# Parts of q and k written by the compute engines straight into the score tiles

## The chip, the cores and the metric

The kernel runs on one core of one Trainium2 chip. The metric is the device time of one execution in microseconds. A core has five engines that run their own in-order queues beside each other: TensorE (PE in the profile, with PEld for its weight loads), VectorE (DVE), ScalarE (ACT), GpSimd (POOL) and SyncE (SP), which here issues all DMA transfers.

## The reference

Attention with rotary embedding, then two MLPs, all in float32:

```python
# q, k, v: batch 4, heads 8, seq 576, head_dim 64
q_rot, k_rot = rotate(q), rotate(k)   # x1*cos - x2*sin, x1*sin + x2*cos
scores = (1 / sqrt(64)) * q_rot @ k_rot.T
attn = softmax(scores)                # over keys, 1e-9 added to the sum
x = (attn @ v) as [2304 tokens, 512]
h = x @ w_in                          # w_in 512 x 2048
g = where(h >= 1, h, where(h <= -1, 0, (h + 1)**2 / 4))
x = g @ w_out                         # w_out 2048 x 512
r = maximum(x @ w_in2, 0)
out = (s * r * r + b) @ w_out2
```

## The kernel before

**Two parts for each number.** TensorE multiplies in a format that rounds float32 (`F32R`). So each operand is split into a high part, the value rounded to that format, and a low part, the rest, and a product is the sum of three: high by high, high by low, low by high.

**Pairs.** Two heads make a pair (`NPAIR` = 16). One head has 64 rows (its head dimension), so a pair's q and k lie in 128 rows, head 0 in rows 0 to 63 (`D` = 64) and head 1 in rows 64 to 127. Columns are the 576 positions. `load_qk` brings q or k of a pair into a tile `qin` or `kin` (one tag, four buffers) as two planes: the value and the value with its halves swapped. `rope_pair` multiplies both planes with the table (L240), adds them (L242), and makes the high part into plane 0 (ScalarE, L244 for q with the factor 1/8, L247 for k) and the low part into plane 1 (L245 on VectorE for q, L248 for k). The products are GpSimd's, except those of the first two pairs' q and the first pair's k; the sum is VectorE's for q and GpSimd's for k (VectorE's for the first k). `pool_tt` cuts GpSimd's work into pieces of at most 300 columns.

**The stacks.** A score matmul contracts over all 128 rows. For each head j the tile `qs` holds q's high part in 64 rows and its low part in the other 64, `kh` holds k's high part twice, once in each half, and `kz` holds k's low part against q's high part and zeros against q's low part. So `kh` by `qs` gives two of the three products in one pass, and `kz` by `qs` the third. `stack` fills these tiles with transfers from SBUF to SBUF of 64 rows by 576 columns: four for q (L259), six for k (L266). There are two `qs`, two `kz` and two buffers of `kh`, so the tiles of pair i + 2 are those of pair i.

**Units.** A pair has nine score tiles (units). For each, `qk` runs the score matmuls into one of two PSUM tiles `sc` (L287), VectorE takes the negated maximum `nm` (L289), and ScalarE the exp `p` (L294) with its sum. `tmain` and `trem` transpose `p` on TensorE and copy it back to SBUF, `finish` multiplies with v and with the inverse sums. `do_load` prepares later pairs: at unit 0 of pair i it traces `rope_pair` for q of pair i + 1, at unit 2 that for k, at units 4 and 6 the loads of pair i + 2.

**Order.** A scheduler of the framework orders each engine's queue beforehand, from a planned timeline; the engines then run their queues in order and wait on semaphores. `tc.issue_after(first)` keeps what is traced under it behind the instruction `first` in its engine's queue: the loads of pair 1 and all that SyncE issues for the first 36 units stand behind the last transfer of the first pair's stacks.

**Around it.** While attention runs, `do_fill` puts parts of the first MLP (`beside`: tiles `h`, `y`) between the units from unit 48 on, and `convert` splits weights (tiles `wraw`, `wa`, `wm`, `w`). The rest of both MLPs follows in `stage` (tiles `hps`, `yps`).

## Time and profile before

| | |
|---|---|
| median of 3 runs | 1181.76 us (1180.75 to 1182.14) |
| the profiled execution | 1180.8 us, its span 1179.0 us |
| TensorE busy | 1116.0 us, 95% of the span |
| ScalarE, VectorE, GpSimd busy | 681.2, 591.5, 557.4 us |
| mean granted TensorE clock | 0.984 of full speed |

The span runs from the first to the last instruction; times in the trace count from its start. Attention's last score matmuls run at about 460 us. Busy shares are averages over stages with different limits, so they are read by stage. "Idle before" an instruction is the idle time of its engine ahead of it, with what ended it. A granted clock of 1.00 is TensorE's 2.4 GHz level, 0.50 its 1.2 GHz level.

### The profile page before, as it was taken

What the parts mean: (1) busy time and instruction counts of PE and PEld (TensorE: products, weight loads), DVE (VectorE), ACT (ScalarE), POOL (GpSimd) and SP (SyncE); (2) the same over time, 40 slices, a digit from 0 to 9 for tenths busy, and PEclk for the clock granted to TensorE, in tenths of its full rate; (3) what the DMA queues carried; (4) which work ended last, traced back from release to release, by engine and by line L of the source; (5) the groups of instructions that cost most, each with busy time, mean ns of one, the idle gap of its engine ahead of it and who ended that gap; (6) DMA issues with size and microseconds to landing.
All of it is one profiled execution on the core that took longest, in us unless ns stands there. A gap on an engine that the chain in (4) does not pass through costs nothing.

```text
span 1179.0 us, 18887 instructions
## 1 busy us (share of the span) xinstructions
PE 1116.0 (95%) x6816; PEld 1001.7 (85%) x6816; DVE 591.5 (50%) x1013; ACT 681.2 (58%) x1431; POOL 557.4 (47%) x712
## 2 busy tenths in 40 slices
PE   3889899899999999999999889999999999999998
PEld 3667677788888888998999889999888889988887
DVE  4769887776554454466655656654411111211221
ACT  2657666655665655566655545567755646555553
POOL 3977987684433110567678887466611110111000
PEclk9989899999999999999999999999999999999999
DMA  7867656655444410433345463444302111312220
GB/s 222 231 179 223 184 156 197 189 159 159 133 141 117 113 52 32 146 118 123 112 154 156 129 179 120 135 135 130 123 33 64 50 41 40 97 33 74 65 65 33
DMA packets 73853, 142.67 MB, mean 121 GB/s; under 512 B 9504, under 2 KB 47392, under 8 KB 73760
## 3 DMA queue, kind: packets, MB, share of 16 engines
q1 hardware_dynamic: 73760, 141.46, 40.2%
q8 instruction: 54, 0.88, 0.3%
q14 instruction: 39, 0.32, 0.1%
HBM read 91.29 MB, written 26.54 MB: 100 GB/s over the span
## 4 chain that ended last, share of the span: by engine, by line
PE 60%; POOL 14%; DMA 7%; issue 6%; DVE 5%; ACT 4%; SPq 3%; POOLq 0%; ACTq 0%; DVEq 0%
PE hps L144 20%; PE yps L574 7%; PE yps L575 7%; PE yps L573 7%; PE sc L287 4%; PE h L144 4%; PE y L144 3%; POOL wm L86 3%; DMA xs<-xd 3%; PE av L335 3%; PE tp L309 3%; POOL kin L86 3%; POOL w L86 3%; POOL xl L86 2%; POOL qin L86 2%
## 5 line engine op out<-in xcount | busy, mean ns | idle before, releaser
L144 PE MATMUL hps<-xh,w 128*128 128x464 f32 (+5 forms) x1216 | 344.6, 349 | 0.8 <-POOL w L86 0.8
L86 POOL TENSOR_TENSOR xl<-xs,xh 128x232 fp32r<-128x232 f32 (+5 forms) x172 | 133.4, 801 | 271.7 <-ACT xh L90 270.5
L144 PEld LDWEIGHTS hps<-xh,w 128*128 128x128 f32 x1216 | 221.8, 188 | 16.0 <-POOL w L86 1.1
L573 PE MATMUL yps<-gh,w 128*128 128x464 f32 (+5 forms) x608 | 213.4, 351 | 4.6 <-ACT yo L580 4.2
L574 PE MATMUL yps<-gl,w 128*128 128x464 f32 (+5 forms) x608 | 212.7, 350 | 5.0 <-DVE gl L94 5.0
L575 PE MATMUL yps<-gh,w 128*128 128x464 f32 (+5 forms) x608 | 212.5, 350 | 0.0
L144 PE MATMUL hps<-xl,w 128*128 128x464 f32 (+5 forms) x608 | 211.5, 348 | 0.5 <-POOL xl L86 0.5
L94 DVE TENSOR_TENSOR gl<-ar,gh 128x464 fp32r<-128x464 f32 (+1 forms) x80 | 56.7, 709 | 268.7 <-ACT gh L90 268.6
L86 POOL TENSOR_TENSOR wm<-wm,w 128x256 f32<-128x256 f32 x128 | 114.8, 917 | 116.5 <-ACT w L131 60.7
L287 PE MATMUL sc<-kh,qs 128*128 128x288 f32 (+2 forms) x384 | 114.1, 332 | 42.3 <-ACT p L294 24.5
L289 DVE TENSOR_REDUCE nm<-sc 128x1 f32<-128x576 f32 x144 | 107.7, 753 | 79.8 <-PE sc L287 79.6
L573 PEld LDWEIGHTS yps<-gh,w 128*128 128x128 f32 x608 | 114.5, 188 | 14.6 <-ACT yo L580 6.3
L574 PEld LDWEIGHTS yps<-gl,w 128*128 128x128 f32 x608 | 114.6, 189 | 13.5 <-DVE gl L94 5.9
L144 PEld LDWEIGHTS hps<-xl,w 128*128 128x128 f32 x608 | 114.3, 188 | 8.3 <-POOL xl L86 0.7
L575 PEld LDWEIGHTS yps<-gh,w 128*128 128x128 f32 x608 | 114.6, 189 | 7.5
L294 ACT ACTIVATE p<-sc,nm 128x576 f32<-128x576 f32 x144 | 106.9, 745 | 23.5 <-DVE nm L289 22.7
L287 PEld LDWEIGHTS sc<-kh,qs 128*128 128x128 f32 x384 | 73.5, 204 | 54.4 <-ACT p L294 32.6
L175 ACT ACTIVATE ar<-hps 128x464 f32<-128x464 f32 (+1 forms) x80 | 44.4, 555 | 129.7 <-PE hps L144 129.7
L287 PE MATMUL sc<-kz,qs 128*128 128x288 f32 (+2 forms) x384 | 102.5, 303 | 0.0
L86 POOL TENSOR_TENSOR w<-wm,wa 128x256 fp32r<-128x256 f32 x128 | 98.3, 785 | 0.0
L94 DVE TENSOR_TENSOR gl<-ac,gh 128x288 fp32r<-128x288 f32 (+3 forms) x112 | 78.9, 706 | 36.3 <-ACT gh L90 34.8
L309 PE MATMUL tp<-ident,p 128*128 128x128 f32 x576 | 92.1, 285 | 0.0
(77 smaller groups left out, 1963.2 us busy)
## 6 DMA issues: line engine op xcount, KB each, us to landing
wraw<-in_ww SPq DMA_DIRECT2D x64, 512.0 KB, 3.9
kh<-kin SPq DMA_DIRECT2D x64, 144.0 KB, 2.6
qs<-qin SPq DMA_DIRECT2D x64, 144.0 KB, 2.6
kin<-in_k SPq DMA_DIRECT2D x15, 576.0 KB, 4.9
qin<-in_q SPq DMA_DIRECT2D x15, 576.0 KB, 4.6
xs<-y1d SPq DMA_DIRECT2D x32, 232.0 KB, 2.6
xs<-xd SPq DMA_DIRECT2D x44, 144.0 KB, 2.4
yd<-ys SPq DMA_DIRECT2D x40, 144.0 KB, 2.1
```

Source lines behind the costliest of these rows:

```text
L86: nc.gpsimd.tensor_tensor(out=out[c], in0=in0[c], in1=in1[c], op=op)
L94: tt(out=dst_lo, in0=src, in1=dst_hi, op=ALU.subtract)
L144: m = nc.tensor.matmul(out_ps, l, r, start=(i == 0), stop=(i == n - 1))
L175: nc.scalar.activation(r, h, AF.Relu)
L287: nc.tensor.matmul(sc[:, half, o:o + n], l, r[:, k0:k0 + n], start=m == 0, stop=m == len(todo) - 1)
L289: nc.vector.tensor_reduce(out=nm, in_=sc[:, :, :288], axis=AX.XY, op=ALU.max, negate=True)
L294: exps[i * 9 + k] = nc.scalar.activation(p, sc[:, :, :288], AF.Exp, bias=nm, scale=1.0, accum_out=sums_t[i][:, col:col + 1]).ins
L309: nc.tensor.transpose(v[:, c, :], p[:, c * P:(c + 1) * P], ident)
L335: nc.tensor.matmul(ps[j * D:(j + 1) * D, :n], v[:, kt, j, :], pt[g][:, kt, j, :], start=kt == 0, stop=False)
L573: nc.tensor.matmul(acc, wh, gh, start=f == 0, stop=False)
L574: nc.tensor.matmul(acc, wh, gl, start=False, stop=False)
L575: nc.tensor.matmul(acc, wl, gh, start=False, stop=last)
```

## The change

`stack` and its ten transfers per pair are gone. `rope_pair` calls `lay_q` or `lay_k` for each piece of columns. Each works on one head (64 rows) at a time. For q, ScalarE writes the high part into the head's own rows of `qs`, and VectorE writes the low part from there into the other 64 rows. For k, ScalarE writes the high part into the head's own rows of `kh`, one transfer copies it to the other 64 rows, and the low part goes into the head's own rows of `kz`: on GpSimd for head 0, and on VectorE for head 1 (on GpSimd for both in the first pair). So every cast and low part is now two instructions of 64 rows instead of one of 128. The zeros of `kz` and the order of the halves for head 1 are changed to suit. `first` is now the last transfer of the first pair's k.

```diff
@@ -205,7 +205,7 @@
     def bank(name):
         return ps_b.tile([P, 512], F32, tag="bank", name=name)
 
-    qk_in, v_in, stacks, parts_t = {}, {}, {}, {}
+    qk_in, v_in, stacks = {}, {}, {}
 
     WHOLE = [slice(0, S)]
     HALVES = [slice(0, 288), slice(288, S)]
@@ -229,41 +229,44 @@
     kz_t = [att.tile([P, 2, S], F32R, name=f"kz{n}") for n in range(2)]
     for n in range(2):
         nc.gpsimd.memset(qs_t[n][:, S:QW].bitcast(F32), 0.0)
-        nc.gpsimd.memset(kz_t[n][D:].bitcast(F32), 0.0)
+        nc.gpsimd.memset(kz_t[n][D:, 0].bitcast(F32), 0.0)
+        nc.gpsimd.memset(kz_t[n][:D, 1].bitcast(F32), 0.0)
 
     def rope_pair(i, nm, mul, add, lo_eng, pieces=WHOLE):
 
         t = qk_in.pop((nm, i))
-        hi, lo = t[:, 0, :].bitcast(F32R), t[:, 1, :].bitcast(F32R)
         tt = {nc.gpsimd: pool_tt, nc.vector: nc.vector.tensor_tensor}
+        last = None
         for c in pieces:
             tt[mul](out=t[:, :, c], in0=t[:, :, c], in1=tab_sb[:, :, c], op=ALU.mult)
             r = t[:, 1, c]
             tt[add](out=r, in0=t[:, 0, c], in1=r, op=ALU.add)
-            if nm == "q":
-                nc.scalar.activation(hi[:, c], r, AF.Copy, scale=0.125)
-                nc.vector.scalar_tensor_tensor(out=lo[:, c], in0=r, scalar=0.125, in1=t[:, 0, c], op0=ALU.mult, op1=ALU.subtract)
-            else:
-                nc.scalar.copy(hi[:, c], r)
-                tt[lo_eng](out=lo[:, c], in0=r, in1=t[:, 0, c], op=ALU.subtract)
-        parts_t[nm, i] = t
-        if i > 0:
-            stack(i, nm)
-
-    def stack(i, nm):
-        t = parts_t.pop((nm, i))
-        if nm == "q":
-            st = stacks["q", i] = qs_t[i % 2]
-            for j in range(2):
-                for a in range(2):
-                    m = nc.sync.dma_start(out=st[a * D:(a + 1) * D, j * QW:j * QW + S].bitcast(F32), in_=t[j * D:(j + 1) * D, a, :])
-            return m.ins
-        kh = att.tile([P, 2, S], F32R, tag="kh", name="kh", bufs=2)
-        kz = kz_t[i % 2]
-        stacks["k", i] = kh, kz
+            last = (lay_q if nm == "q" else lay_k)(i, t, c, lo_eng)
+        return last
+
+    SELF = [slice(0, D), slice(D, P)]
+
+    def lay_q(i, t, c, lo_eng):
+
+        st = stacks["q", i] = qs_t[i % 2]
+        r = t[:, 1, c]
         for j in range(2):
-            for st, a, o in ((kh, 0, 0), (kh, 0, D), (kz, 1, 0)):
-                m = nc.sync.dma_start(out=st[o:o + D, j, :].bitcast(F32), in_=t[j * D:(j + 1) * D, a, :])
+            own, other = SELF[j], SELF[1 - j]
+            at = slice(j * QW + c.start, j * QW + c.stop)
+            nc.scalar.activation(st[own, at], r[own], AF.Copy, scale=0.125)
+            nc.vector.scalar_tensor_tensor(out=st[other, at], in0=r[own], scalar=0.125, in1=st[own, at], op0=ALU.mult, op1=ALU.subtract)
+
+    def lay_k(i, t, c, lo_engs):
+        if c.start == 0:
+            stacks["k", i] = att.tile([P, 2, S], F32R, tag="kh", name="kh", bufs=2), kz_t[i % 2]
+        kh, kz = stacks["k", i]
+        tt = {nc.gpsimd: pool_tt, nc.vector: nc.vector.tensor_tensor}
+        r = t[:, 1, c]
+        for j in range(2):
+            own, other = SELF[j], SELF[1 - j]
+            nc.scalar.copy(kh[own, j, c], r[own])
+            m = nc.sync.dma_start(out=kh[other, j, c].bitcast(F32), in_=kh[own, j, c].bitcast(F32))
+            tt[lo_engs[j]](out=kz[own, j, c], in0=r[own], in1=kh[own, j, c], op=ALU.subtract)
         return m.ins
 
     UNITS = [(0, 0), (1, 0), (0, 1), (1, 1), (None, 4), (0, 2), (1, 2), (0, 3), (1, 3)]
@@ -418,10 +421,8 @@
         if c is HALVES[0]:
             load_qk(0, "k", HALVES)
     load_qk(0, "q", HALVES)
-    rope_pair(0, "k", nc.vector, nc.vector, nc.gpsimd, HALVES)
-    rope_pair(0, "q", nc.vector, nc.vector, nc.vector, HALVES)
-    stack(0, "k")
-    first = stack(0, "q")
+    first = rope_pair(0, "k", nc.vector, nc.vector, [nc.gpsimd, nc.gpsimd], HALVES)
+    rope_pair(0, "q", nc.vector, nc.vector, None, HALVES)
     with tc.issue_after(first):
         load_qk(1, "k")
         load_qk(1, "q")
@@ -464,9 +465,9 @@
             i, k = units[n]
             if i + 1 < NPAIR:
                 if k == 0:
-                    rope_pair(i + 1, "q", nc.gpsimd if i else nc.vector, nc.vector, nc.vector)
+                    rope_pair(i + 1, "q", nc.gpsimd if i else nc.vector, nc.vector, None)
                 elif k == 2:
-                    rope_pair(i + 1, "k", nc.gpsimd, nc.gpsimd, nc.gpsimd)
+                    rope_pair(i + 1, "k", nc.gpsimd, nc.gpsimd, [nc.gpsimd, nc.vector])
                 elif k == 3:
                     load_v(i + 1)
                 elif k in (4, 6) and i + 2 < NPAIR:
```

## Rows read from the trace of the kernel before

**Rows 1.** The page's head.

```profile
span 1179.0 us, 18887 instructions
```

**Rows 2.** Windows: us, busy PE, PEld, DVE, ACT, POOL; granted clock; DMA share; GB/s.

```profile
20.00:260.00 240.00, 215.50 (x1513) 176.38 (x1512) 189.82 (x333) 152.00 (x353) 190.35 (x228) 0.93 0.66 195
260.00:462.00 202.00, 195.69 (x1521) 172.62 (x1521) 110.80 (x219) 120.61 (x302) 58.70 (x76) 1.00 0.40 112
462.00:1179.00 717.00, 702.40 (x3781) 650.34 (x3777) 284.32 (x454) 405.61 (x772) 303.59 (x397) 1.00 0.31 97
```

**Rows 3.** TensorE by line, 20 to 260 us: busy, mean ns, idle before.

```profile
L287 PE MATMUL sc<-kh,qs 128*128 128x288 f32 (+2 forms) x226 | 70.4, 347 | 21.1 <-ACT p L294 21.1
```

**Rows 4.** Timeline of TensorE, idle times: first, a double one, last.

```profile
35.24 0.40 PE L287 MATMUL sc<-kh,qs 128*128 128x288 f32 x1 [0.69 <-ACT p L294]
...
76.40 0.40 PE L287 MATMUL sc<-kh,qs 128*128 128x288 f32 x1 [2.45 <-ACT p L294]
...
79.05 0.77 PE L287 MATMUL sc<-kh,qs 128*128 128x64 f32 x2 [1.00 <-ACT p L294]
...
235.12 0.77 PE L287 MATMUL sc<-kh,qs 128*128 128x64 f32 x2 [1.08 <-ACT p L294]
```

**Rows 5.** Timeline of VectorE in the pair of that double idle time.

```profile
73.08 1.35 DVE L242 TENSOR_TENSOR qin<-qin 128x576 f32<-128x576 f32 x1 [0.69 <-POOL qin L86]
...
75.35 1.10 DVE L245 SCALAR_TENSOR_TENSOR qin<-qin 128x576 fp32r<-128x576 f32 x1
...
80.79 0.76 DVE L289 TENSOR_REDUCE nm<-sc 128x1 f32<-128x576 f32 x1 [1.83 <-PE sc L287]
...
88.29 0.76 DVE L289 TENSOR_REDUCE nm<-sc 128x1 f32<-128x576 f32 x1 [1.90 <-PE sc L287]
```

**Rows 6.** Timeline of ScalarE in the same pair.

```profile
74.46 0.69 ACT L244 ACTIVATE qin<-qin 128x576 fp32r<-128x576 f32 x1 [2.75 <-DVE qin L242]
...
88.15 0.48 ACT L367 COPY r<-rm 128x384 f32<-128x384 f32 x1 [2.29 <-PE rm L364]
```

**Rows 7.** Window of 3 us behind that double idle time, columns as rows 2.

```profile
80.00:83.00 3.00, 3.00 (x15) 2.97 (x14) 1.15 (x2) 2.03 (x5) 3.00 (x5) 0.50 0.35 77
```

**Rows 8.** Timeline of the first 22 us: start, us, work [idle before].

```profile
10.38 1.17 SPq L266 DMA_DIRECT2D kh<-kin  x2
...
11.57 0.81 ACT L244 ACTIVATE qin<-qin 128x288 fp32r<-128x288 f32 x2 [1.22 <-DVE qin L242]
...
12.04 0.83 DVE L245 SCALAR_TENSOR_TENSOR qin<-qin 128x288 fp32r<-128x288 f32 x2
...
14.21 2.48 SPq L259 DMA_DIRECT2D qs<-qin  x4
16.73 0.59 SPq L217 DMA_DIRECT2D kin<-in_k  x1
...
17.64 0.74 PE L287 MATMUL sc<-kh,qs 128*128 128x64 f32 x2 [17.64 <-DMA qs<-qin]
```

**Rows 9.** The page's DMA issues: count, size, us to landing.

```profile
kh<-kin SPq DMA_DIRECT2D x64, 144.0 KB, 2.6
```

**Rows 10.** VectorE by line, 20 to 260 us, columns as rows 3.

```profile
L245 DVE SCALAR_TENSOR_TENSOR qin<-qin 128x576 fp32r<-128x576 f32 x12 | 12.0, 1002 | 0.1
...
L370 DVE TENSOR_TENSOR u<-av,r 128x256 f32<-128x256 f32 x17 | 7.1, 416 | 5.7 <-ACT r L367 5.5
...
L372 DVE TENSOR_TENSOR u<-av,r 64x64 f32<-64x64 f32 x9 | 1.9, 206 | 0.0
```

**Rows 11.** Who waited for whom in SyncE's queue: total us, times, longest.

```profile
SPq L259 <- PE sc L287: 24.5, 6, 6.4
```

**Rows 12.** Timeline of SyncE's queue around the end of one pair.

```profile
124.00 2.84 SPq L259 DMA_DIRECT2D qs<-qin  x4
...
131.86 0.50 SPq L217 DMA_DIRECT2D qin<-in_q  x1
```

## The prediction

> **What bounds the kernel now.** The profiled execution took 1180.8 us for a span of 1179.0 [rows 1], so 1.8 us lie outside the span; the median of the runs is 1181.76, about 1.0 above the profiled one. I read the windows first [rows 2]. Behind 462 us only the two MLPs run. TensorE is busy there for 702 of 717 us at full clock, and none of it is touched: if attention ends earlier, all of this shifts by as much. From 260 to 462 us TensorE is busy for 196 of 202 us, since MLP work fills its gaps. So attention's early part decides: from 20 to 260 us TensorE stands idle for 24.5 us, and its granted clock is 0.93 on average, worth (1 - 0.93) x 240 = 17 us more. Before 20 us it waits for the first scores.
>
> Next I read the idle times by line [rows 3]: 21.1 of the 24.5 us stand before score matmuls that wait for an exp to free their PSUM tile. The timeline shows where: in the middle of most pairs, twice within 3 us [rows 4]. Fourteen such idle times make 17.9 us; the second ones alone (seven, 0.69 to 1.08 us, of which rows 4 hold the first, one, and the last) make 6.4.
>
> The other engines' timelines say what happens at 73 to 77 us [rows 5, 6]. VectorE waits for GpSimd's products of q (0.69), adds them (1.35), and a little later makes q's low parts (1.10) ahead of the maximum that the next exp needs. ScalarE, in order, stands 2.75 us at the cast of q's high parts, because this waits for VectorE's add. Exps queue behind it, and TensorE behind them. What follows costs as much again: at 80 to 83 us TensorE is busy all the time at a clock of 0.50, the 1.2 GHz level [rows 7]. Six stretches like this lie in the early part, each behind such an idle time, 1.7 to 3.4 us apiece.
>
> **The change, part by part.**
>
> Start. Before, the first scores wait for the last of q's four transfers, issued from 14.21 on, and start at 17.64 [rows 8]. Now q needs no transfer. The last of k's copies can be issued when the cast of k's second piece is done: 10.4 us, where the first copy went out before, with 0.6 apiece for the two heads. Landing takes 2.6 us [rows 9]: 13.0 for head 0, 13.6 for head 1. ScalarE makes four half-height casts of q from 11.57 on, at 0.41 each (the 0.81 of the two there): 13.2. VectorE's four low parts follow at 0.42 each from 12.04 on, the last behind the last cast, and end near 13.7. The first scores start between 13.1 and 13.9: 4.1 us earlier, bounds 3.7 and 4.5. Pair 1's loads stand behind these transfers in SyncE's queue. They go out when the last copy has been issued, at 11.6 instead of 16.73, so they don't hold the gain back.
>
> What a half-height instruction costs. No row shows one of 64 x 576. If rows counted, it would take half as long as 128 x 576; if only columns count, as long. On VectorE 64x64 takes 206 ns and 128x256 takes 416 [rows 10]; 210 ns for 192 columns is 1.09 ns each, and 576 columns at that rate from 416 on would be 765 ns at full height, near the 0.74 to 0.76 of the 128x576 reductions [rows 5]. So the 64-row instruction lies on the line of the 128-row ones: I take the full price. Per pair ScalarE then has two more casts (0.69 each [rows 6], 1.4 us), VectorE one more low part of q (1.00 on average [rows 10]) and one of k (0.75 by the columns, 1.35 as the add beside GpSimd's work [rows 5]; I take 1.0). GpSimd's two instructions for k's low parts stay two: they now hold one head each time at the same width, and VectorE has the other head. Over the 12 q's and 11 k's of the early part VectorE gets 23 us (20 to 27) on top of 189.8 busy of 240, ScalarE some 16 on top of 152 [rows 2].
>
> On the shared access of VectorE and GpSimd the trace has one pair of numbers: q's low part took 1.10 us at 75.35, and 1.00 on average [rows 5, 10], where I would expect some 0.75 from the columns. The Trainium skill (SBUF — State Buffer, section "SBUF: two separate sides") says that a VectorE instruction with two SBUF inputs and a GpSimd instruction that reads SBUF exclude each other for their whole length. By it GpSimd would pay as well for each new VectorE instruction; the sum with that is in the rivals, as the slower one.
>
> Where the work goes. The cast writes the score tile itself, which the pair two before still reads. So it can't run in the middle of a pair any more: it waits for that pair's last scores, and comes at the boundary of two pairs. Two things leave the middle: ScalarE's wait on the cast, and VectorE's low parts ahead of the maximum. VectorE's add, and its wait for GpSimd, stay. So I take the second idle times away, 6.4 us, and keep the first (bounds: nothing, and all 17.9). Of the clock's 17 us I take a third back, 5.7: two of the six slow stretches don't come. The bounds are nothing and 17; a new stretch at a boundary would cost up to 3.4.
>
> At the boundary ScalarE gets four casts (2.7 us) and VectorE three low parts (3.0). TensorE has transposes and the product with V to do there, while VectorE waits for scores for 1.83 and 1.90 us and ScalarE 2.29 [rows 5, 6]. Most is covered; I count 0.6 us per pair as uncovered, ten times: 6 us lost. The bounds are nothing, and all that VectorE gets, 23 (27 by the dear price). Without the cover it is the next pair's exps that are late.
>
> The queue. SyncE issued ten transfers per pair, now two. Around 124 us the next load of q stood behind them from 124.00 to 131.86 [rows 12]; it can go about 4 us earlier, and GpSimd's products with it. I count nothing for that, since the product is made more than a pair ahead; the bound is the rest of the first idle times, which is held in the 17.9. Past 260 us the added work lies beside a busy TensorE, with VectorE at 111 of 202 us [rows 2]: nothing, and without that cover at most some 8 us for four pairs.
>
> Sum: -4.1 (start) - 6.4 (second idle times) - 5.7 (clock) + 6.0 (boundary) = -10.2. 1180.8 - 10.2 = 1170.6 for a profiled execution; as a median, 1.0 more: 1171.6.
>
> **The rivals.**
>
> A wait on ScalarE in place of SyncE's, slower. Before, SyncE held q's transfers until TensorE was through with the tile: 24.5 us in six waits, up to 6.4 [rows 11]. SyncE had little else to do. Now ScalarE's cast has that wait. If it stands in the queue ahead of the old pair's last exp, that exp and the PSUM tile wait with it. All of it on the path: -4.1 + 24.5 = +20, or 1202; half of it, 1190. It decides from the point where 4 of the 24.5 us reach TensorE. For it: the order in a queue is fixed beforehand, from planned times. Against it: the last scores come before the next pair's, so most exps don't stand behind the cast.
>
> VectorE becomes the bound, slower. In 20 to 260 us it would be busy for 210 to 217 of 240. If all of the 23 us come through: -4.1 + 23 = +19, or 1201; with half, 1189. It decides at 1.05 us per pair when nothing is won in the middle but the 6.4. By the skill's rule above GpSimd loses too, which makes this likelier.
>
> The middle is relieved wholly: no idle time and no slow clock there, boundary as counted: -4.1 - 17.9 - 17 + 6 = -33, or 1149. For it: loads come earlier. Against it: VectorE's add remains.
>
> Only the start is won. The added work stalls at the boundary about what the middle gives back: -4.1, or 1177.7. Or the start is eaten too, and the time stays within 0.2%, near 1181.
>
> **How the numbers follow.** 0.2%, 2.4 us, is about what a measurement can tell from no change. My forecast (1163 to 1176): 0.43. Only the start: 0.11. The middle wholly relieved: 0.11. No change: 0.13. VectorE the bound: 0.13. The wait on ScalarE: 0.09. So faster 0.65, same 0.13, slower 0.22. The range from 1158 to 1188 leaves out the far end of the relieved middle (about 0.07) and the upper half of the slower cases (about 0.12).
>
> **What the profile of the changed kernel would show.** Start: the first score matmul between 13 and 14 us, and no transfers into the tile of q. Price: casts and low parts of 64 x 576 at 0.67 to 0.69 and 0.75 to 1.4 us; 0.35 would prove me wrong. Middle: ScalarE's idle time before the cast of q gone, second idle times of TensorE gone, granted clock of 20 to 260 us above 0.93. Boundary: new idle times of score matmuls there, under 1 us each. VectorE as the bound would show as busy for over 92% of the early part, with maxima that wait for nothing; the wait on ScalarE as idle time before casts that ends with a score matmul. The forecast fails if the order in the queues changes so that stalls move to where I have none, or if the clock falls at the boundaries as it fell in the middle.

## The result and the profile after

The changed kernel takes 1186.48 us (median of 9 runs, 1183.19 to 1190.89), the kernel before 1179.38 in the same session (9 runs, 1174.82 to 1182.14). The ratio is 1.0069, with a 95% interval from 1.005 to 1.0088: slower, where faster was forecast. The time lies inside the range of the prediction, on its slow side.

The profiled execution took 1187.14 us. The page's head of the changed kernel:

```profile
span 1185.4 us, 18709 instructions
```

Its windows, columns as in [rows 2]:

```profile
20.00:260.00 240.00, 203.10 (x1441) 164.47 (x1441) 203.27 (x333) 153.33 (x351) 182.23 (x217) 0.93 0.45 139
260.00:462.00 202.00, 195.35 (x1529) 172.94 (x1529) 126.49 (x238) 128.35 (x320) 65.35 (x84) 1.00 0.27 85
```

The span grew by 6.4 us over [rows 1]. From 20 to 260 us TensorE now stands idle for 36.9 us of 240, where it was 24.5 [rows 2]; the granted clock is 0.93 as before. TensorE by line over the same stretch shows that all of the additional idle time stands at the same place as before, score matmuls that wait for an exp; [rows 3] had 21.1 there:

```profile
L290 PE MATMUL sc<-kh,qs 128*128 128x288 f32 (+2 forms) x215 | 65.5, 340 | 35.3 <-ACT p L297 35.3
```

The start went nearly as forecast. The timeline of the first 20 us, to be set beside [rows 8]:

```profile
10.38 1.10 SPq L268 DMA_DIRECT2D kh<-kh  x2
...
11.54 0.58 SPq L217 DMA_DIRECT2D kin<-in_k  x1
11.58 1.88 ACT L256 ACTIVATE qs<-qin 64x288 fp32r<-64x288 f32 x4 [0.78 <-DVE qin L243]
...
12.55 1.91 DVE L257 SCALAR_TENSOR_TENSOR qs<-qin,qs 64x288 fp32r<-64x288 f32 x4
...
13.05 0.77 PE L290 MATMUL sc<-kh,qs 128*128 128x64 f32 x2 [13.05 <-DVE qs L257]
```

The first scores start at 13.05 instead of 17.64, 4.6 us earlier. They no longer wait for a transfer, only for the first of VectorE's four low parts of q. The first exp stands at 15.59 (before 20.14). But that of pair 1 stands at 44.20 (41.69), and the last exp of attention starts at 466.71 (460.76). So 10.5 us are lost between the first and the last exp, 7.1 of them in pair 0 alone.

What happens in pair 0 is one instruction. Timelines of GpSimd, VectorE, ScalarE and TensorE around 30 us in the changed kernel:

```profile
26.97 1.54 POOL L86 TENSOR_TENSOR kz<-kin,kh 64x288 fp32r<-64x288 f32 x2
28.47 3.03 POOL L86 TENSOR_TENSOR kin<-kin,tab_sb 128x288 f32<-128x288 f32 x4
31.46 1.30 POOL L86 TENSOR_TENSOR kin<-kin 128x288 f32<-128x288 f32 x1
...
27.05 5.07 DVE L243 TENSOR_TENSOR qin<-qin 128x576 f32<-128x576 f32 x1 [0.76 <-POOL qin L86]
32.05 0.74 DVE L292 TENSOR_REDUCE nm<-sc 128x1 f32<-128x576 f32 x1
...
32.88 0.74 ACT L297 ACTIVATE p<-sc,nm 128x576 f32<-128x576 f32 x1 [5.34 <-DVE sume L354]
...
33.77 0.77 PE L290 MATMUL sc<-kh,qs 128*128 128x64 f32 x2 [6.52 <-ACT p L297]
```

VectorE's add of q, 1.35 us in [rows 5], takes 5.07 here. It starts beside GpSimd's two instructions for k's low part of head 0 and ends only in the last of the seven instructions that GpSimd runs back to back. The maximum, the exp and the scores queue behind it: ScalarE idle 5.34, TensorE 6.52. What such an idle time costs behind itself is as before [rows 7]; the windows from 29 us show the 1.2 GHz level (0.50), which lasts until about 40 us, 6 us past the end of the idle time:

```profile
29.00:32.00 3.00, 0.00 (x0) 0.00 (x0) 3.00 (x1) 0.00 (x0) 3.00 (x5) 0.60 0.65 226
32.00:35.00 3.00, 1.23 (x5) 1.23 (x6) 2.64 (x7) 1.66 (x4) 1.49 (x3) 0.50 0.00 0
35.00:38.00 3.00, 3.00 (x14) 2.70 (x13) 2.43 (x3) 2.30 (x5) 3.00 (x4) 0.50 0.02 5
```

A second kind of loss stands at the boundaries of pairs, where TensorE's idle times were 0.2 to 0.3 us and are now 1.78, 2.38, 2.58 and 2.86 us (at 66.79, 90.11, 113.92 and 138.27). Around 110 us in the changed kernel:

```profile
106.52 2.14 POOL L86 TENSOR_TENSOR kz<-kin,kh 64x288 fp32r<-64x288 f32 x2 [3.52 <-ACT kh L267]
...
108.05 1.24 DVE L257 SCALAR_TENSOR_TENSOR qs<-qin,qs 64x576 fp32r<-64x576 f32 x1
...
111.59 0.68 DVE L352 TENSOR_SCALAR sume<-sums 128x4 f32<-128x4 f32 x1
112.19 0.74 DVE L292 TENSOR_REDUCE nm<-sc 128x1 f32<-128x576 f32 x1
...
113.92 0.48 PE L290 MATMUL sc<-kh,qs 128*128 128x64 f32 x2 [2.58 <-ACT p L297]
```

Low parts of q, of k and a small sum stand ahead of the new pair's first maximum, and the low part of q beside GpSimd's work is long: 1.24 us where the one at 104.93 took 0.75.

### The profile page after: what moved, and what is told of

It is laid out like the page before. It is cut to its first block, busy times and chain, and to the rows that moved or that the text cites. A ratio compares the mean times of both kernels' runs of the same rounds, so it can differ in the third digit from the quotient of the medians.

```text
span 1185.4 us, 18709 instructions
## 1 busy us (share of the span) xinstructions
PE 1114.5 (94%) x6816; PEld 1000.1 (84%) x6816; DVE 629.5 (53%) x1045; ACT 698.5 (59%) x1465; POOL 562.8 (47%) x716
## 4 chain that ended last, share of the span: by engine, by line
PE 63%; DVE 12%; POOL 9%; DMA 5%; ACT 5%; issue 4%; SPq 1%; POOLq 0%; ACTq 0%; DVEq 0%
PE hps L144 21%; PE yps L575 7%; PE yps L576 7%; PE yps L574 7%; PE sc L290 5%; PE h L144 4%; PE y L144 4%; PE av L338 3%; PE tp L312 3%; DMA xs<-xd 2%; POOL wm L86 2%; POOL w L86 2%; DVE nm L292 2%; POOL xl L86 2%; DVE wm L128 2%
## 5 line engine op out<-in xcount | busy, mean ns | idle before, releaser
L86 POOL TENSOR_TENSOR wm<-wm,w 128x256 f32<-128x256 f32 x128 | 118.9, 948 | 110.0 <-ACT w L131 54.6
```

Source lines behind the costliest of these rows:

```text
L86: nc.gpsimd.tensor_tensor(out=out[c], in0=in0[c], in1=in1[c], op=op)
```

## The experiments

In what follows the theories have letters, as the expectations use them. **A**: the boundary. Casts and low parts go into tiles that the pair before still reads, so they pile up between two pairs. **B**: the one long add at 27 us by itself, behind back-to-back GpSimd work that the earlier start put there. **C**: VectorE has too much to do. **D**: GpSimd's instructions of 64 rows make VectorE wait for many GpSimd instructions instead of one; at first any such instruction, later only an unequal number on the two halves, as in the changed kernel (two on the lower 64 rows for head 0, none on the upper). **E**: VectorE and GpSimd work on k's low parts at the same boundary and block each other at the usual size. All medians are in us, each beside runs of the kernel before on the same chip; the last column counts VectorE instructions of more than 2 us in the profiled execution, up to the last exp of attention.

```
kernel                                             median   ratio  95% interval     long
changed kernel                                    1186.48  1.0069  1.0050..1.0088     1
e1 first pair only                                1173.54  0.9955  0.9927..0.9984     0
e2 q direct, k by transfers                       1172.23  0.9951  0.9930..0.9971     0
e3 k direct, q by transfers                       1184.75  1.0048  1.0013..1.0082     4
e4 three tiles for q                              1174.89  0.9961  0.9940..0.9981     2
e8 three tiles for q, k by transfers              1172.42  0.9942  0.9914..0.9970     0
e5 both low parts of k on GpSimd                  1169.95  0.9917  0.9886..0.9948     1
e6 both low parts of k on VectorE                 1173.40  0.9959  0.9934..0.9983     0
f1 low parts shared out by columns                1180.17  1.0011  0.9993..1.0030     0
f3 on GpSimd, the two halves meant to alternate   1173.36  0.9945  0.9922..0.9969     1
f2a before + two unread GpSimd instr., lower      1189.73  1.0100  1.0058..1.0143     3
f2b before + the same, one lower, one upper       1181.37  1.0035  1.0012..1.0058     0
g1 e6 + two unread, one lower, one upper          1181.32  1.0028  1.0010..1.0046     0
g2 e6 + two unread, both lower                    1184.17  1.0045  1.0026..1.0064     2
g3 heads exchanged between the engines            1174.30  0.9966  0.9948..0.9983     0
g4 head 1 first                                   1191.24  1.0106  1.0071..1.0141     4
g5 head 1 first, heads exchanged                  1179.21  1.0008  0.9986..1.0030     0
```

**Which part of the change costs.** Three kernels undo it for k, for q, or for both from pair 1 on; what is undone goes through the tile and SyncE's transfers as before.

```diff
     def lay_k(i, t, c, lo_engs):
+        if i > 0:      # e1 and e2; the same in lay_q for e1 and e3
+            hi, lo = t[:, 0, c].bitcast(F32R), t[:, 1, c].bitcast(F32R)
+            nc.scalar.copy(hi, t[:, 1, c])
+            pool_tt(out=lo, in0=t[:, 1, c], in1=t[:, 0, c], op=ALU.subtract)
...
+                    m = nc.sync.dma_start(out=st[o, j, :].bitcast(F32), in_=t[SELF[j], a, :])
```

e1_first_only. Expected: 

> Only the first pair is written directly; pairs 1 to 15 go back to the transfers, in the changed layout. Theory A (the casts and low parts of later pairs wait for the scores two pairs before and come in one burst at the boundary of two pairs, where the next maxima stand behind them) and theory C (VectorE's added work by itself): the start's 4.6 us are kept and the stalls at boundaries are gone: ratio to the kernel before 0.996, some 1175 us. Theory B (the one add that took 5.07 us at 27 us, behind back-to-back GpSimd work that the earlier start put there, is what costs): the long add comes again, since the start is the same, and the ratio stays at 1.001 to 1.006.

e2_q_direct. Expected: 

> q is written directly for all pairs, k by transfers from pair 1 on, its low parts whole on GpSimd. Theory A: the burst at a boundary is halved (two casts and two low parts of q stay), its idle times fall from 2.4 to about 1 us: 1180 us, ratio 1.000. Theory C: 12 of the 13 us that VectorE gained for k's low parts are gone, the 11 us for q stay: ratio 1.002. Theory B: ratio 1.001 to 1.006 if the long add comes again, 0.997 if not.

e3_k_direct. Expected: 

> k is written directly for all pairs, q by transfers from pair 1 on, its low part one instruction of 128 rows. Theory A: at the boundary two casts and one low part of k stay on ScalarE and VectorE; idle times of about 1 us there, and q's cast and low part are back in the middle with their idle times: 1181 us, ratio 1.002. Theory C: some 8 us of VectorE's growth are gone: ratio 1.003. Theory B: as with q direct, by whether the long add comes.

Measured 0.9955, 0.9951 and 1.0048. The first pair alone brings 5 us; q for all pairs neither adds nor takes anything that these intervals show; k for all pairs is where it is lost. In e1 and e2 the start is the same as in the changed kernel and no long instruction comes, so the earlier start alone (B) isn't what brings it. In e3, timelines of GpSimd, VectorE and TensorE show the same thing as above, larger:

```profile
43.89 2.07 POOL L86 TENSOR_TENSOR kz<-kin,kh 64x288 fp32r<-64x288 f32 x2
...
46.81 8.02 DVE L254 SCALAR_TENSOR_TENSOR qin<-qin 128x576 fp32r<-128x576 f32 x1
...
56.48 0.61 PE L299 MATMUL sc<-kh,qs 128*128 128x288 f32 x1 [5.55 <-ACT p L306]
```

GpSimd ran eleven more instructions back to back, from 45.92 to 54.2; VectorE's low part of q, about 1 us in [rows 10], came to its end at 54.83, after the last of them.

**Boundary, amount of work, or GpSimd (A, C, D).** A third tile for q lets the casts go a pair earlier (for its room, 128 columns that nothing reads are cut off each); e8 has it with k by transfers. e5 and e6 give k's low parts to one engine.

```diff
-    qs_t = [att.tile([P, 2 * QW], F32R, name=f"qs{n}") for n in range(2)]
+    qs_t = [att.tile([P, 2 * QW - 2 * D], F32R, name=f"qs{n}") for n in range(3)]    # e4, e8
...
-                    rope_pair(i + 1, "k", nc.gpsimd, nc.gpsimd, [nc.gpsimd, nc.vector])
+                    rope_pair(i + 1, "k", nc.gpsimd, nc.gpsimd, [nc.gpsimd, nc.gpsimd])    # e5
+                    rope_pair(i + 1, "k", nc.gpsimd, nc.gpsimd, [nc.vector, nc.vector])    # e6
```

e4_three_qs. Expected: 

> The changed kernel with three score tiles of q in place of two (128 unused columns behind each are cut to make room), so that q's casts and low parts of pair i + 2 don't wait for the scores of pair i, with the same instructions. Theory A: q's part leaves the boundary, idle times there fall from 2.4 to about 1 us, time between 1176 and 1181, ratio 0.997 to 1.002. Theory C: the same work on VectorE, no gain: ratio 1.006. Theory B: ratio 1.006 if the long add comes again, 0.998 if the order changes and it doesn't.

e8_three_qs_kmove. Expected: 

> q written directly into three tiles in turn, k by transfers from pair 1 on: both of the versions that beat the kernel before, in one. Theory D: no GpSimd instruction of 64 rows after the first pair, no long VectorE instruction, and q's casts free of the boundary: ratio 0.990 to 0.994. Theory A: the same or better than either alone, 0.991 to 0.995. If three tiles only helped by moving the long instructions about, they add nothing to q direct with transfers of k: 0.995.

e5_lo_gpsimd. Expected: 

> The changed kernel with k's low parts of both heads on GpSimd: four instructions of 64 x 288 per pair there instead of two, and none of VectorE's fifteen. Theory C and theory A: VectorE has some 18 us less to do, half the burst: ratio to the kernel before 0.999 to 1.002. Theory D: GpSimd has more instructions of 64 rows, but as many for the upper rows as for the lower; long VectorE instructions come again if any GpSimd instruction of 64 rows brings them (ratio 1.004 to 1.008), and not if only unequal numbers for the two halves do (ratio as theory C).

e6_lo_vector. Expected: 

> The changed kernel with k's low parts of both heads on VectorE from pair 1 on, so that GpSimd has no instruction of 64 rows any more after the first pair, while VectorE gets one more instruction of 64 x 576 per pair (15 in all, some 1.2 us each). Theory C (VectorE's added work is what costs) and theory A (the burst at the boundary): slower than the changed kernel by 5 to 12 us, ratio to the kernel before 1.010 to 1.016. Theory D (a VectorE instruction with two SBUF inputs that meets back-to-back GpSimd work behind GpSimd instructions of 64 rows waits for several of them): no VectorE instruction over 2 us is left except at the start, the 6.5 us idle time at 33 us and the slow clock behind it go away: ratio 0.997 to 1.002.

Measured 0.9961, 0.9942, 0.9917 and 0.9959. e6 decides against C: VectorE has one more low part per pair and is busy for 209.9 of 240 us, and the kernel gains 0.4%. It also decides against A as the main cause, since all the writing to the tiles stays where it was. e5 says the same from the other side, and is the fastest version of all: 0.9917, faster than both kernels and than any theory expected. Either engine alone does; the two together, as the changed kernel divides k's low parts, don't. e4 doesn't fit a single cause: a third tile brings 1.1% although two long VectorE instructions (5.07 and 2.69) are still there. With k by transfers (e8) it brings nothing that the intervals show over e2 (0.9942 against 0.9951).

**The wait by itself (D).** A kernel of its own runs nine GpSimd adds of 128 x 288 back to back and a VectorE add of 128 x 576 with two SBUF inputs beside them; ahead of them stand no, one, two or four GpSimd adds of 64 rows. It computes nothing of the reference.

```diff
+            for n, rows in enumerate(front):
+                nc.gpsimd.tensor_tensor(out=side[rows, ...], in0=x[rows], in1=gout[0][rows], op=ALU.add)
+            for n in range(1, 10):
+                nc.gpsimd.tensor_tensor(out=gout[n], in0=x, in1=y, op=ALU.add)
+            nc.vector.tensor_tensor(out=res[0], in0=gout[1][:, :1].to_broadcast([P, S]), in1=src[:, 1, :], op=ALU.add)
```

m1_shared_port. Expected: 

> A kernel of its own that computes nothing of the reference: GpSimd runs nine additions of 128 x 288 back to back, and VectorE makes four additions of 128 x 576 with two SBUF inputs beside them. Ahead of the nine stand on GpSimd, by variant: nothing (va), one 64-row addition on the lower rows (vb), two of them (vc), one on the lower and one on the upper rows (vd), two and two (ve), one of 128 rows (vf). Each variant runs three times. Theory D: VectorE's additions take 1.3 us at most in va, vf, and several microseconds in vb and vc; vd and ve tell whether equal halves cure it. Theory C: the same 0.75 to 1.4 us in all.

VectorE by line, the first add of each case, three times each: nothing ahead (va), one lower (vb), two lower (vc), one lower and one upper (vd):

```profile
L84 DVE TENSOR_TENSOR vc<-g,src 128x576 f32<-128x576 f32 x3 | 17.5, 5820 | 7.9 <-POOL g L83 7.9
...
L84 DVE TENSOR_TENSOR vb<-g,src 128x576 f32<-128x576 f32 x3 | 4.2, 1388 | 5.7 <-POOL g L83 5.7
...
L84 DVE TENSOR_TENSOR va<-g,src 128x576 f32<-128x576 f32 x3 | 4.0, 1328 | 4.2 <-POOL g L83 4.2
L84 DVE TENSOR_TENSOR vd<-g,src 128x576 f32<-128x576 f32 x3 | 4.0, 1327 | 8.6 <-POOL g L83 8.6
```

Beside GpSimd the add takes 1.33 us, near the 1.35 of [rows 5]. With two lower GpSimd instructions ahead it takes 5.82, all three times: six or so instructions of GpSimd instead of one. GpSimd's nine then take 7.28 us, otherwise 8.83. One lower instruction was expected to do it too, but leaves the add at 1.39. Two lower and then two upper ones (ve) or one of 128 rows (vf) leave it at 1.33.

**The wait in the kernels (D, and its control).** f1 shares each low part out by columns, so that GpSimd gets one instruction on each half; f3 has all on GpSimd, lower and upper meant to alternate. f2a and f2b are the kernel before with two GpSimd instructions per pair whose result nobody reads.

```diff
+                for e, p in zip((pool_tt, nc.vector.tensor_tensor), HALVES):    # f1
+                    e(out=kz[own, j, p], in0=r[own, p], in1=kh[own, j, p], op=ALU.subtract)
...
+        for p in ([c] if i == 0 else HALVES):                                   # f3
+            for j in range(2):
+                pool_tt(out=kz[SELF[j], j, p], in0=t[SELF[j], 1, p], in1=kh[SELF[j], j, p], op=ALU.subtract)
...
+                    for rows in (slice(0, D), slice(0, D)):                     # f2a; f2b: (0, D), (D, P)
+                        nc.gpsimd.tensor_tensor(out=dum[rows], in0=t[rows, 0, :288], in1=tab_sb[rows, 0, :288], op=ALU.subtract)
```

f1_halves. Expected: 

> The changed kernel with the same division of k's low parts between the two engines, cut the other way: for each head GpSimd makes the first 288 columns and VectorE the rest, so that GpSimd has one instruction on the lower rows and one on the upper rows instead of two on the lower, and VectorE two of 288 columns instead of one of 576. Theory D (only unequal numbers of 64-row instructions on GpSimd's two halves let VectorE wait for several instructions): no VectorE instruction over 2 us, ratio to the kernel before 0.992 to 1.000. Theories A and C (place and amount of VectorE's work, both unchanged): ratio 1.004 to 1.009, as the changed kernel.

f3_lo_in_turn. Expected: 

> k's low parts of both heads on GpSimd, as in the fastest run so far, but in turn: lower rows, upper rows, lower, upper, after both casts. Theory D: the one VectorE instruction of 3.6 us that was left there is gone too, ratio 0.989 to 0.993. Without theory D: no difference to that run, 0.992, or worse, since the first low part now waits for the second cast as well.

f2a_lower. Expected: 

> The kernel before, with two GpSimd instructions of 64 x 288 more per pair from pair 1 on, both on the lower rows, whose result nothing reads. Theory D: VectorE instructions of 2 to 8 us appear, which the kernel before doesn't have, and the time grows by 5 to 15 us: ratio 1.004 to 1.013. Without theory D: 1.6 us more of GpSimd's work per pair, as in the control with one instruction on each half: 1.000 to 1.005.

f2b_both. Expected: 

> The control: the kernel before with two GpSimd instructions of 64 x 288 more per pair, one on the lower and one on the upper rows. Theory D: no VectorE instruction over 2 us; ratio 1.000 to 1.005 and below that with both on the lower rows by at least 0.003. Without theory D: the same ratio as with both on the lower rows.

f1 came to 1.0011 with no long instruction, so most of the loss goes (1.0069 to 1.0011, some 7 us), but not all that e5 and e6 win. In the kernel before, two lower instructions per pair cost 1.0% and bring three VectorE instructions of 2.1 to 2.9 us; one lower and one upper cost 0.35% and bring none. The two intervals touch, and the half isn't all that differs: in f2a the scheduler put other GpSimd instructions between the two, in f2b not. f3 missed its expectation that no long one would be left. The reason is in the instruction list: the scheduler didn't keep the alternation. GpSimd's tensor-tensor instructions from the start on, "L" lower 64 rows, "U" upper, "." 128 rows (the trace gives the number of rows; which half follows from the program and from the time of two in a row, 1.53 us on one half and 1.63 for a lower and an upper one in m1):

```
changed   LULU..........LL...................LL......LL...............LL
f3, e5    LULU..........LL...UU...............LLUU......LLUU............
g1        LULU..........L...U............L...U........LU..............LU
g3        LULU.............UU...............UU........UU..............UU
g4        LULU.............LL...............LL........LL..............LL
```

f3 and e5 have the same list here, and in both the one long add falls between the two lower instructions and the two upper ones that follow later. In f3, where the two instructions of a half take 1.53 and 1.54 us together, GpSimd and VectorE:

```profile
28.23 1.53 POOL L86 TENSOR_TENSOR kz<-kin,kh 64x288 fp32r<-64x288 f32 x2
...
32.59 1.54 POOL L86 TENSOR_TENSOR kz<-kin,kh 64x288 fp32r<-64x288 f32 x2
...
28.30 3.57 DVE L243 TENSOR_TENSOR qin<-qin 128x576 f32<-128x576 f32 x1 [3.03 <-POOL qin L86]
```

**Presence against halves.** g1 and g2 hold VectorE's work fixed (that of e6) and add the two unread GpSimd instructions.

```diff
+            if i > 0:                  # g1; g2: if i > 0 and j == 0, for both HALVES
+                nc.gpsimd.tensor_tensor(out=dum[own], in0=r[own, :288], in1=kh[own, j, :288].bitcast(F32), op=ALU.subtract)
```

g1_both. Expected: 

> The version with both of k's low parts on VectorE (0.9959 of before), and beside them two GpSimd instructions per pair whose result nobody reads, 64 x 288 each: one on the lower 64 rows behind the cast of head 0, one on the upper 64 behind that of head 1. GpSimd has as much to do at that place as in the changed kernel, in equal numbers on both halves. Theory E, the two engines at work on k's low parts at the same boundary of pairs is what the rest of the loss consists of: up by about 0.5%, to 1.000 to 1.002, as with k's low parts shared out by columns (1.0011), without a VectorE instruction over 2 us. Theory D alone, only an unequal number on the two halves counts: 0.994 to 0.998, as without them.

g2_lower. Expected: 

> The same with both unread GpSimd instructions on the lower 64 rows, behind the cast of head 0, as GpSimd's own part lies in the changed kernel. Theory D: VectorE instructions of 2 to 6 us come back and the time goes to 1.004 to 1.010, at least 0.4% above the version with one on each half. Theory E alone: as that version, within 0.2%.

Their mere presence at that place costs 0.7% (0.9959 to 1.0028, the intervals apart), which speaks for E. Both on the lower rows bring two long instructions back, of 4.58 and 2.47 us, but the times, 1.0028 and 1.0045, have overlapping intervals: the 0.4% that D asked for wasn't there.

**Which half, or which order.** g3 exchanges the heads between the engines, which changes both the half GpSimd works on and who comes first; g4 and g5 turn the order round.

```diff
-                    rope_pair(i + 1, "k", nc.gpsimd, nc.gpsimd, [nc.gpsimd, nc.vector])
+                    rope_pair(i + 1, "k", nc.gpsimd, nc.gpsimd, [nc.vector, nc.gpsimd])    # g3, g5
...
-        for j in range(2):
+        for j in (0, 1) if i == 0 else (1, 0):                                            # g4, g5
```

g3_swap. Expected: 

> The changed kernel with the heads exchanged: VectorE makes k's low part of head 0, GpSimd that of head 1, two instructions on the upper 64 rows and none on the lower. Theory D in its general form, any unequal number on the two halves: VectorE instructions of 2 to 6 us as in the changed kernel, 1.004 to 1.010. If only the lower rows do it: none over 2 us, and 0.999 to 1.003, as shared out by columns. Should the order of the two engines at the boundary decide instead (VectorE's part now comes first), the time lies below 1.000.

g4_order. Expected: 

> The changed kernel with the two heads of k worked on in the other order from pair 1 on: cast, copy and low part of head 1 (VectorE) first, then those of head 0 (GpSimd, two instructions on the lower 64 rows, none on the upper). Each engine has what it has in the changed kernel. If GpSimd's uneven number on the lower rows is what costs: VectorE instructions of 2 to 6 us stay, 1.003 to 1.009. If the order decides (GpSimd's part first, so that VectorE's low part and what follows it meet it): none over 2 us, and 0.995 to 0.999, as with the heads exchanged.

g5_order_swap. Expected: 

> The same order (head 1 first), with the heads exchanged between the engines: GpSimd makes the low part of head 1 first, two instructions on the upper rows, then VectorE that of head 0. If the lower rows are what costs: no VectorE instruction over 2 us, 0.995 to 0.999, as with the heads exchanged in the old order (0.9966). If the order decides: long instructions, 1.003 to 1.009.

m2_halves. Expected: 

> A kernel that computes nothing of the reference: nine GpSimd adds of 128 x 288 back to back and a VectorE add of 128 x 576 beside them, as in the earlier measurement, with other GpSimd instructions of 64 rows ahead: none (va), two on the lower rows (vc), two on the upper (vg), four lower (vh), four upper (vi), two lower and one upper (vj), two upper and then two lower (vk). If any uneven number of two or more counts: vc, vg, vh and vi above 5 us, va, vj and vk near 1.33. If only more on the lower rows count: vg and vi also near 1.33. If the delay grows with the surplus, vh is longer than vc, up to the nine instructions' whole length of some 7.3 us.

```
GpSimd's low part of k       comes first              comes after VectorE's
on the lower 64 rows         1.0069 (1 long)          1.0106 (4 long)
on the upper 64 rows         1.0008 (none)            0.9966 (none)
```

The same work costs 0.6% or 1.4% more when GpSimd has the lower rows, in either order and with the intervals apart. Long instructions in attention come with the lower rows alone. D in the form "any uneven number" falls, as does "the order decides"; g4 and g5 lie some 0.2% above the ranges that were expected for the lower rows as the cause, and g3 lay 0.2% below its own. The exchange also moves VectorE's part to the other half; in m1 and m2 VectorE's add has 128 rows throughout, so there GpSimd's half is enough for the long wait. In g4, timelines of VectorE and GpSimd show the longest of all, beside a run of GpSimd that has no pause from 27.28 to 40.7:

```profile
32.14 7.93 DVE L257 SCALAR_TENSOR_TENSOR qs<-qin,qs 64x576 fp32r<-64x576 f32 x1
...
30.04 1.55 POOL L86 TENSOR_TENSOR kz<-kin,kh 64x288 fp32r<-64x288 f32 x2
...
37.16 3.56 POOL L86 TENSOR_TENSOR kin<-kin,tab_sb 128x288 f32<-128x288 f32 x4
```

The order by itself shows only where nothing is long: 1.0008 against 0.9966, with the intervals just apart; 1.0069 and 1.0106 have overlapping ones. Where nothing is long, VectorE's low part of k takes 1100 ns on average behind GpSimd's part (g5, 20 to 260 us) and 828 ns ahead of it (g3), in line with E; in the changed kernel it takes 1165. m2, VectorE by line, two upper ahead (vg), two lower and one upper (vj), two upper and then two lower (vk); of the four lower (vh) and four upper ones (vi) that were meant to stand ahead, see below:

```profile
L84 DVE TENSOR_TENSOR vk<-g,src 128x576 f32<-128x576 f32 x3 | 17.5, 5820 | 12.8 <-POOL g L83 12.8
...
L84 DVE TENSOR_TENSOR vh<-g,src 128x576 f32<-128x576 f32 x3 | 17.5, 5819 | 7.9 <-POOL g L83 7.9
...
L84 DVE TENSOR_TENSOR vj<-g,src 128x576 f32<-128x576 f32 x3 | 4.0, 1328 | 15.1 <-POOL g L83 15.1
L84 DVE TENSOR_TENSOR vi<-g,src 128x576 f32<-128x576 f32 x3 | 4.0, 1328 | 8.5 <-POOL g L83 8.5
L84 DVE TENSOR_TENSOR vg<-g,src 128x576 f32<-128x576 f32 x3 | 4.0, 1328 | 8.3 <-POOL g L83 8.3
```

Equal numbers are not what helps: vk has two of each and takes 5.82. What counts is what came last. Two lower ones with no upper one behind them bring the long wait; a single upper one afterwards ends it. Whether four are worse than two was not measured: the scheduler put the second two of vh behind the nine adds (those of vi as well), as GpSimd's timeline shows:

```profile
36.23 1.53 POOL L81 TENSOR_TENSOR side<-src,g 64x288 f32<-64x288 f32 x2
37.73 7.28 POOL L83 TENSOR_TENSOR g<-src,g 128x288 f32<-128x288 f32 x9
44.97 2.56 POOL L81 TENSOR_TENSOR side<-src,g 64x288 f32<-64x288 f32 x2
```

With that reading all seventeen kernels of the table fit in one respect, up to the last exp of attention: every one that shows an instruction of more than 2 us has such a stretch in its list (in g2 and f2a with instructions of 128 rows between the two), and those without one show none. The stretch is not enough by itself: the changed kernel has one in each pair and one long instruction. In m2 the condition doesn't outlast a pause: the case with nothing ahead (va) twice follows vk's two lower ones after 2.5 us of idle time and a copy of 128 x 8, and takes 1.33.

It is not the only way to a long wait either. Behind attention, at about 700 us, VectorE's first weight instruction (L127) takes 3.86 to 3.88 us in six profiled executions: those of the kernel before, the changed kernel, e3, f1, f3 and g3. GpSimd has only adds of 128 rows there. In the kernel before, GpSimd and VectorE:

```profile
701.10 4.39 POOL L86 TENSOR_TENSOR yo<-yo,yp 128x184 f32<-128x184 f32 x8
...
701.90 3.87 DVE L127 TENSOR_SCALAR wm<-wa 128x512 uint32<-128x512 uint32 x1 [2.36 <-ACT wa L126]
```

At the same place it takes 0.63 us in e1. From the last exp to the end it is 718.0 to 719.5 us in the six executions and 715.5 to 717.4 in the other twelve, so some 2 us come and go that no edit here aims at. What starts this wait is not shown, and the long L127 instructions of g4 and f2a may be of its kind.

## Why the prediction was wrong

**The step that failed** is the price of VectorE's two-input instructions beside GpSimd, in "What a half-height instruction costs": 1.0 us, with 1.35 as the upper bound, and with it the sentence that "GpSimd's two instructions for k's low parts stay two", which cost them at nothing. The bound came from [rows 5], and those rows hold no GpSimd instruction on half of the rows, because the kernel before has none on tensors of q and k. The change puts two on the lower rows in each pair and none on the upper, and VectorE's instructions beside GpSimd's runs then take up to 5.07 us (8.02 in e3). The miss is some 18 us (1.0069 against the 0.991 forecast). Leaving every count and size of the change as it was, GpSimd's move to the upper rows takes back 7 of them (g5, 1.0008), and VectorE's part ahead of GpSimd's another 5 (g3, 0.9966). The profiled executions of the changed kernel and of g5 show where the 7 lie: 6.1 us between the first and the last exp, 5.0 of them in pair 0, where the long add stands (28.6 us against 23.6). The other 6 us of the miss are the terms of the middle and the boundary, below.

The Trainium skill (SBUF — State Buffer, section "SBUF: two separate sides") says that whichever starts first has the shared access "for the whole instruction". The 1.33 us in m1 agree with a wait for one GpSimd instruction; the 5.82 do not, and there the measurement decides.

**Start, -4.1**: nearly right, -4.6 in the profiled execution, 0.1 beyond its bound of 4.5. The prediction let the scores wait for the last of VectorE's four low parts; they wait for the first. It is kept in the other versions of the changed kernel: first exps lie between 15.6 and 16.4 us.

**Half-height instructions at full price**: right. ScalarE's casts of 64 x 576 take 682 and 665 ns on average, VectorE's low parts 0.75 us where GpSimd doesn't work, 948 (q) and 1165 ns (k) on average from 20 to 260 us. VectorE is busy for 203.3 of 240 us; 210 to 217 were forecast, for the 12 q's and 11 k's of the kernel before, and the slower kernel makes 10 of each in that time.

**Middle, -6.4 and -5.7, boundary, +6.0**: wrong even without the long waits. ScalarE's wait on the cast is gone from the middle, as foreseen, but the second idle times that were to go with it are not: they stand at 56.82, 79.53, 103.12, 127.22, 152.99 and 243.49 in the changed kernel, 1.08 us each. The prediction put them down to the cast and the low parts. In the changed kernel neither runs from 98 to 104 us; timelines of TensorE and ScalarE there:

```profile
103.12 0.48 PE L290 MATMUL sc<-kh,qs 128*128 128x64 f32 x2 [1.08 <-ACT p L297]
...
101.75 0.58 ACT L314 COPY pt<-tp 128x512 f32<-128x512 f32 x1 [1.05 <-PE tp L312]
102.23 0.75 ACT L297 ACTIVATE p<-sc,nm 128x576 f32<-128x576 f32 x1
```

The exp that TensorE waits for stands in ScalarE's queue behind the copy of a transposed `p`, and this waits 1.05 us for TensorE's transposes. In the kernel before it was so already at 79.05 [rows 4], where ScalarE shows:

```profile
77.68 0.59 ACT L311 COPY pt<-tp 128x512 f32<-128x512 f32 x1 [1.05 <-PE tp L309]
```

Three of the seven second idle times of the kernel before had this copy ahead of their exp (54.65, 79.05 and 235.12, 3.2 of the 6.4 us) and were not the change's to win. The other four had the cast ahead; with the cast gone, the wait for the transposes is what is left. The clock gave nothing back either: 0.93 in the early part before and after. At the boundaries the new idle times are 1.78 to 2.86 us where less than 1 was foreseen, and still up to 2.40 in g3, which has no long wait. The idle times before scores are longer in sum than in [rows 3] in g3 (30.8 us) and e6 (27.6) too. g3, e6 and e2 end where e1 ends, which writes the first pair alone: 0.995 to 0.997. So what the middle gives and what the boundary takes come out about equal there, where -6.1 was forecast, and the case "only the start is won" is what is left of the change once GpSimd's half and the order are put right.

**The rivals.** VectorE as the bound ended on the right side for the wrong reason: e6 gives it more work and is faster. The wait on ScalarE is small: casts of q and k wait for scores for 1.4 and 0.8 us in the whole early part, not half of 24.5. The queue moved as foreseen: pair 1's load of k goes out at 11.54 (11.6 forecast).

**What stays open.** Most of the first 7 us lie where the one long instruction stands, but e5 loses 5.6 us in pair 0 with a long add of 3.61 and is the fastest nevertheless. The 5 us between g5 and g3 have no such place: g3's pair 0 is 1.4 us longer than g5's, and its gain is spread over later pairs. Why a third tile for q makes up for the loss (e4) was not taken further. Why GpSimd's two instructions cost 0.7% in g1 without a long wait is explained by E only as far as the averages go.

## What to carry to other kernels

Where GpSimd and VectorE work side by side, look at which rows an instruction covers, not only at how many it has: work on half of the rows cost as much as work on all of them, and two GpSimd instructions on rows 0 to 63 slowed VectorE long after they had ended. Where this shows, give the lower rows to VectorE or let an upper one follow at once, and read the order in the instruction list, since a scheduler can undo an order written in the source. A transfer that is removed pays where its latency stands in front of everything, here in the first pair; where transfers ran beside other work, the instructions that replace them have to be paid, here on a VectorE that was already 79% busy (189.8 of 240 us). And before an idle time is put down to the instruction that the change removes, look at what stands last ahead of it in the waiting engine's queue.

## What the runs showed of the hardware

- Two GpSimd adds of 64 x 288 on rows 0 to 63, last before a run of GpSimd adds, make a VectorE add with two SBUF inputs take 5.82 us instead of 1.33, six times out of six in two kernels; on rows 64 to 127 they don't (1.328), nor with an upper one behind them (1.328). One lower one alone: 1.39. The condition outlasts GpSimd instructions of 128 rows, but not a pause of 2.5 us with a copy of 128 x 8 (1.33 again in m2).
- A VectorE instruction with a single tensor input can be held as long: the TENSOR_SCALAR at L127 took 3.87 us in the kernel before, beside a GpSimd run of 128 rows; at the same place in e1 it took 0.63. In g4 it took 4.83 and 5.78 us beside GpSimd's runs. What starts this is not shown.
- GpSimd's instruction of 64 x 288 takes 782 ns at the least, as long as one of 128 x 288 (0.79 at 32.31 in g4).
